# One load of w_down rows split in two, its lower half on eight DMA engines, with the FFN columns permuted to match

## The chip, the cores and the metric

The kernel runs on one core of a Trainium2 chip. The metric is the device time in microseconds (us), measured over whole executions; the profile is of one of these executions. The time before is 188.97 us, the median of 3 runs (188.87 to 189.1).

## The reference

One decode step of a transformer block with adaptive layer norm, for two rows (B = 2, one token each) of width D = 640, in bfloat16. Cut to what matters:

```python
mod = (silu(c) @ w_mod).reshape(2, 6, 1, 640)          # sa, ca, ga, sb, cb, gb
h = layernorm(x) * (1 + ca) + sa
q = (h @ wq) as 32 heads of 192
scores = q @ k_cache[:, :, -1024:].T * 192 ** -0.5
o = softmax(scores) @ v_cache[:, :, -1024:]
x = x + ga * (o @ wo)
h = layernorm(x) * (1 + cb) + sb
x = x + gb * ((gelu(h @ w_gate) * (h @ w_up)) @ w_down) # w_gate, w_up: 640 x 1536; w_down: 1536 x 640
```

The weights and the used part of the caches are 77 MB, each byte of which is used for two rows at most: all of it must come from HBM once.

## The kernel before, in words

The program is written as a list of operations, each for one engine (TensorE "pe", VectorE "dve", ScalarE "act", GpSimd "pool", SyncE "sp"), with the buffers that it reads and writes. A small scheduler works out from these which semaphores each operation waits for, and emits each engine's list in the order in which it was written. It moves nothing: the order of the work is that of the text.

All large loads are issued by SyncE, through one helper (`k_dma`, L266), in this order: w_mod; two pieces of wq; then K and V of 16 groups (four heads of one batch row each) in turn, through a ring of eight slots; three pieces of wo; then w_gate, two pieces of w_up (`WU_SPLIT`), four pieces of w_down (`WD_SPLIT`); and at the very end the store of the result. The FFN weights go to the buffer `r3`, which held w_mod before. Each load covers 128 partitions; each piece has a semaphore of its own, which a DMA raises by 16 in all.

The attention part multiplies K by q on VectorE (L490), sums on TensorE by matmuls with an identity matrix (L502), takes the softmax on VectorE and ScalarE, and multiplies by V on TensorE (L551). wo follows (L622), then the second layer norm (from L392 on).

The FFN is what the change touches. The F = 1536 hidden columns are dealt out as `f = 12 p + r`: partition p of w_down's buffer `wd_v` holds its rows 12 p to 12 p + 11, so that each load takes whole runs of a partition's rows; a piece of `WD_SPLIT` is (first r, count): rows 9 to 11 first, then 0 to 4, 5 to 7, and 8. Gate and up (function `ffn_gu`, matmuls at L655) have to put hidden column `12 p + r` where the transpose will bring it to partition p. They run over five k steps of 128; in each, four matmuls of 384 columns, in four column groups of the array (`tile_position`), make the columns `r = 3 i` to `3 i + 2` of all 128 p for i = 0 to 3: their order within group i is `(m r)`, m being p. ScalarE takes GELU of gate (L661), VectorE multiplies by up (L664), `a_T` (L672) transposes with twelve matmuls, VectorE copies the result to `aT` (L676). Then w_down (L684): for each of its pieces and each row number `fc` in it, four matmuls of 160 columns, which accumulate over all twelve `fc`. VectorE scales (L689) and adds the residual (L691), and SyncE stores.

So the engines' order at the end is, on TensorE: gate; up, first piece (three k steps); up, second piece (two k steps); `a_T`; `down0` to `down3`, each waiting for its own piece. `HP` is 64, `FR` is 3, `FC` is 12, `NR` is 4 and `FT` is 384.

Of the kernel before, what the change touches and what calls it, by code (L numbers as in the profile page):

```python
# [119 lines left out]
def bass_adaLN_cond__sliding_block_cached__geglu_ffn__decode_kernel(  # L120
# [14 lines left out]
    P = 128  # L135
    B, _, D = A_x.shape
# [4 lines left out]
    KT = D // P  # L141
    NQ = H * Dh
    NR = 4
# [8 lines left out]
    FR = 3  # L152
    FC = F // P
# [23 lines left out]
    HP = P // 2  # L177
# [4 lines left out]
    FT = F // NR  # L182
# [4 lines left out]
    with es:  # L187
        S = _Sched(nc, es)
# [40 lines left out]
        h2T = sb("h2T", [P, KT, B], BF16)  # L229
# [11 lines left out]
        aT = sb("aT", [P, FC, RM], BF16)  # L241
        fin = sb("fin", [P, DR], F32)
        finb = sb("finb", [P, DR], BF16)
        ps = es.enter_context(nc.psum_tensor("ps", [P, 8, 512], F32))
# [3 lines left out]
        BK_OT = 6  # L248
# [4 lines left out]
        def bank(k):  # L253
            return ("bank", k)
# [5 lines left out]
        sem_wu = [S.sem("d_wu%d" % i) for i in range(len(WU_SPLIT))]  # L260
        sem_wd = [S.sem("d_wd%d" % i) for i in range(len(WD_SPLIT))]
        sem_ring = [S.sem("d_ring%d" % i) for i in range(NS)]
        sem_out = S.sem("d_out")

        def k_dma(dst, src):
            return lambda e: e.dma_start(dst, src)  # L266
# [11 lines left out]
        for it in items:  # L278
            m = nslots.get(it, 1)
# [27 lines left out]
        def declare_ring(consumed=()):  # L307
            ring_state["done"].update(consumed)
            while ring_state["next"] < len(items):
                it = items[ring_state["next"]]  # L310
                if not all(h in ring_state["done"] for h in before_of[it]):
# [7 lines left out]
                       writes=["wm"], name="ld_wm")  # L319
# [4 lines left out]
        for nm, t in (("scT", scT), ("oT", oT), ("aT", aT)):  # L324
# [6 lines left out]
             reads=["ones_f"], writes=["ident_f"], name="ident_f")  # L331
        S.op("pool", lambda e: e.tensor_copy(out=ident_b[:, :], in_=ident_f[:, :]),
             reads=["ident_f"], writes=["ident_b"], name="ident_b")
# [3 lines left out]
             reads=["ones_b"], writes=["selrow"], name="selrow")  # L337
# [3 lines left out]
             reads=["ones_b"], writes=["selg"], name="selg")  # L341
        for b in range(B):
# [4 lines left out]
                 reads=["ones_b"], writes=[("selq", b)], name="selq%d" % b)  # L347
# [4 lines left out]
             reads=["ones_b"], writes=["ztmp"], name="ztmp")  # L352
# [6 lines left out]
             reads=["ones_f", "bcL"], writes=["bcL"], name="bcLh")  # L359
# [5 lines left out]
             reads=["bcR"], writes=["bcR"] + [("bcR", z) for z in range(2)], name="bcRd")  # L365
# [4 lines left out]
             reads=["ident_f"], writes=["mask_h"], name="mask_h")  # L370
        S.op("dve", lambda e: e.tensor_reduce(out=st32[:, :], in_=ident_f[:, :].rearrange("p (i m) -> p m i", m=32), axis=AX.X, op=ALU.add),
             reads=["ident_f"], writes=["st32"], name="st32")
# [3 lines left out]
             reads=["st32"], writes=["selstat"], name="selstat")  # L376
# [3 lines left out]
        def c_T(e):  # L380
            last = None
            for j in range(KT):
# [4 lines left out]
             reads=[bank(BK_T)], writes=["scT"], name="silu")  # L387
        S.op("dve", lambda e: e.tensor_copy(out=X[:, :], in_=xr[:, :]),
             reads=["xr"], writes=["X"], name="x_f32")
# [20 lines left out]
        def ln_mod(tag, opc_idx, s_idx, dst_bf):  # L410
# [7 lines left out]
            def f(e):  # L418
# [14 lines left out]
             reads=["mask_h"], writes=["maskc"], name="maskc")  # L433
        S.op("dve", lambda e: e.tensor_reduce(out=zsel[:, :, X0:X0 + P].rearrange("p q (h m) -> p q h m", m=32)[:, :, :, 0],
                                              in_=ztmp[:, :, :, :].rearrange("p i q h -> p q h i"), axis=AX.X, op=ALU.max),
             reads=["ztmp", "zsel"], writes=["zsel"], name="zsel")

        mod_pe = []
        for half in range(2):
            def f(e, half=half):  # L440
                last = None
                for k in range(KT):
                    wv = wm_v[:, k, :].rearrange("p (m i n) -> p m i n", i=NR, n=DR)
                    for i in range(NR):
                        last = e.matmul(ps[32 * i:32 * i + RM, half, 0:MH].rearrange("p (m n) -> p m n", n=DR), lhsT=scT[:, k, :],  # L445
                                        rhs=wv[:, 3 * half:3 * half + 3, i, :],
                                        start=(k == 0), stop=(k == KT - 1), tile_position=(0, 32 * i))
                return last
# [3 lines left out]
                 reads=[bank(half)], writes=[("modR", half)], name="mod%d_evac" % half)  # L452
            S.op("dve", lambda e, half=half: e.tensor_scalar(out=opc[:, half, :], in0=modR[:, 3 * half + 1, :], scalar1=1.0, scalar2=None, op0=ALU.add),
                 reads=[("modR", half)], writes=[("opc", half)], name="opc%d" % half)
# [17 lines left out]
        for n in range(NQB):  # L472
            if n % 2 == 0:
                S.op("act", lambda e, n=n: e.activation(out=qrow[:, n * QW:(n + 1) * QW], in_=ps[:, n, :], func=ACTF.Copy),  # L474
                     reads=[bank(n)], writes=[("qrow", n)], name="q1_evac%d" % n)
            else:
                S.op("dve", lambda e, n=n: e.tensor_copy(out=qrow[:, n * QW:(n + 1) * QW], in_=ps[:, n, :]),  # L477
                     reads=[bank(n)], writes=[("qrow", n)], name="q1_evac%d" % n)
        for u, (n, b) in enumerate((n, b) for n in range(NQB) for b in range(B)):
            bk = BK_T + u % 4  # L480
            S.op("pe", lambda e, n=n, b=b, bk=bk: e.matmul(ps[:, bk, :], lhsT=selq[:, b, :], rhs=qrow[:, n * QW:(n + 1) * QW], start=True, stop=True),
                 reads=[("selq", b), ("qrow", n)], writes=[bank(bk)], name="q2_%d_%d" % (n, b))
            S.op("act", lambda e, n=n, b=b, bk=bk: e.activation(out=qbc[:, b, n * QW:(n + 1) * QW], in_=ps[:, bk, :], func=ACTF.Copy),  # L483
                 reads=[bank(bk)], writes=[("qbc", b, n)], name="q2_evac%d_%d" % (n, b))
# [98 lines left out]
        for g in range(NG + 2):  # L583
# [23 lines left out]
            if prev:  # L607
# [5 lines left out]
             reads=[bank(BK_OT)], writes=["oT"], name="oT")  # L613
        for ci, (t0, n) in enumerate(WO_SPLIT):
            def f(e, ci=ci, t0=t0, n=n):
# [13 lines left out]
        r3_dead = [wm_dma] + mod_pe  # L629
        S.dma("sp", k_dma(wg_v.rearrange("p k n -> p (k n)"), B_w_gate.rearrange("(p k) n -> p (k n)", k=KT)), sem_wg,  # L630
              writes=["wg"], deps=r3_dead, name="ld_wg")
        for ci, (k0, nk) in enumerate(WU_SPLIT):
            S.dma("sp", k_dma(wu_v[:, k0:k0 + nk, :].rearrange("p k n -> p (k n)"), B_w_up.rearrange("(p k) n -> p (k n)", k=KT)[:, k0 * F:(k0 + nk) * F]), sem_wu[ci],
                  writes=[("wu", ci)], deps=r3_dead, name="ld_wu%d" % ci)
        wd_src = B_w_down.rearrange("(p r) n -> p (r n)", r=FC)
        for ci, (r0, nr) in enumerate(WD_SPLIT):
            dst, src = wd_v[:, r0:r0 + nr, :].rearrange("p r n -> p (r n)"), wd_src[:, r0 * D:(r0 + nr) * D]
            S.dma("sp", k_dma(dst, src), sem_wd[ci], writes=[("wd", ci)], deps=r3_dead, name="ld_wd%d" % ci)

        S.op("dve", lambda e: e.memset(ps[:, 0:2, :], 0.0), writes=[bank(0), bank(1)], name="init_G")  # L640
        S.op("dve", lambda e: e.tensor_tensor(out=lnt[:, :], in0=ps[:, BK_M, 0:DR], in1=modR[:, 2, :], op=ALU.mult),  # L641
             reads=[bank(BK_M), ("modR", 0)], writes=["lnt"], name="ga_attn")
        S.op("dve", lambda e: e.tensor_tensor(out=X[:, :], in0=lnt[:, :], in1=X[:, :], op=ALU.add),
             reads=["lnt", "X"], writes=["X"], name="x1")
# [3 lines left out]
        def ffn_gu(bk, wv, name, splits):  # L648
            for ci, (k0, nk, key) in enumerate(splits):
                def f(e, k0=k0, nk=nk):  # L650
                    last = None
                    for k in range(k0, k0 + nk):
                        wk = wv[:, k, :].rearrange("p (m i r) -> p i m r", i=NR, r=FR)
                        for i in range(NR):
                            last = e.matmul(ps[32 * i:32 * i + B, bk, 0:FT].rearrange("p (m r) -> p m r", r=FR), lhsT=h2T[:, k, :],  # L655
                                            rhs=wk[:, i, :, :], start=(k == 0), stop=(k == KT - 1), tile_position=(0, 32 * i))
                    return last
                S.op("pe", f, reads=["ln2_out", key], writes=[bank(bk)], name="ffn_%s%d" % (name, ci))

# [2 lines left out]
             reads=[bank(0)], writes=["gl"], name="gelu")  # L662
        ffn_gu(1, wu_v, "up", [(k0, nk, ("wu", ci)) for ci, (k0, nk) in enumerate(WU_SPLIT)])
        S.op("dve", lambda e: e.tensor_tensor(out=aR[:, :], in0=ps[:, 1, 0:FT], in1=gl[:, :], op=ALU.mult),  # L664
             reads=[bank(1), "gl"], writes=["aR"], name="geglu")

        def a_T(e):
            last = None
            for i in range(NR):
# [7 lines left out]
             reads=[bank(2)], writes=["aT"], name="aT")  # L677
        for ci, (r0, nr) in enumerate(WD_SPLIT):
            def f(e, r0=r0, nr=nr):
                last = None  # L680
                for fc in range(r0, r0 + nr):
                    wv = wd_v[:, fc, :].rearrange("p (i n) -> p i n", i=NR)
                    for i in range(NR):
                        last = e.matmul(ps[32 * i:32 * i + RM, BK_OT, CY:CY + DR], lhsT=aT[:, fc, :], rhs=wv[:, i, :],  # L684
                                        start=(fc == WD_SPLIT[0][0]), stop=(fc == WD_SPLIT[-1][0]), tile_position=(0, 32 * i))
                return last
            S.op("pe", f, reads=["aT"] + [("wd", ci)], writes=[bank(BK_OT)], name="down%d" % ci)

        S.op("dve", lambda e: e.tensor_tensor(out=fin[:, :], in0=ps[:, BK_OT, CY:CY + DR], in1=modR[:, 5, :], op=ALU.mult),  # L689
             reads=[bank(BK_OT), ("modR", 1)], writes=["fin"], name="gb_y")  # L690
        S.op("dve", lambda e: e.tensor_tensor(out=finb[:, :], in0=fin[:, :], in1=X[:, :], op=ALU.add),  # L691
             reads=["fin", "X"], writes=["finb"], name="outR")
        S.dma("sp", k_dma(out[:, 0, :].rearrange("b (i n) -> i b n", i=NR), finb[0:P:RB, :]),
              sem_out, reads=["finb"], name="st_out")
# [35 lines left out]
```

## Time and profile before

| | |
|---|---|
| median of 3 runs | 188.97 us (188.87 to 189.1) |
| the profiled execution's own time | 188.87 us |
| its span, first to last instruction | 187.6 us |
| moved by DMA | 77.03 MB, mean 411 GB/s |
| TensorE busy | 107.5 us (57%), 1039 matmuls, mean granted clock 0.901 |
| VectorE busy | 98.2 us (52%) |
| ScalarE busy | 29.9 us (16%) |
| load of w_down rows 9 to 11, 5 to 7: 480 KB each | 30.6 us from issue to landing (median of the two) |
| gate matmuls | 175.51, for 1.89 us |
| last DVE step, then the store's issue | 185.52, then 185.87 |

How to read it: the span is what the profiler saw between the first and the last instruction; the time of an execution is a little longer, since something lies around the span. "Busy" is the time in which an engine had an instruction running; with three engines half busy or more, shares alone do not tell what sets the end. The chain of work that ended last does: it goes back from the last instruction, at each step to what released it. In a line of the timeline the columns are the start and the duration in us, the engine, the line of the kernel, the operation and its operands, the number of instructions merged, and in brackets how long the engine had been idle before and what ended that. A load's time "to landing" runs from its issue to the last of the 16 increments of its semaphore, and includes its time in the queue behind earlier loads.

### The profile page before, as it was taken

The page shows a single profiled execution, that of the slowest core. Times are in us where ns is not written, and L with a number is a line of the kernel's source. Part 1 is how long each engine was busy: PE and PEld are TensorE (multiplying, and loading weights), DVE is VectorE, ACT ScalarE, POOL GpSimd, SP SyncE. Part 2 cuts the span into 40 slices and gives each one's busy share as a digit, 9 for nine tenths or more (in the row PEclk, how much of TensorE's full clock was granted, in tenths as well). Part 3 has the DMA queues.
Part 4 walks back from the last instruction along what each step waited for, and adds up shares of the span by engine and source line. Part 5 has one row for each costly group of instructions (what it writes and reads, how often), then busy time and mean ns, then how long its engine had stood idle before and what let it go on. Part 6 is the DMA issues. An engine that isn't in the chain of part 4 may idle for free.

```text
span 187.6 us, 2409 instructions
## 1 busy us (share of the span) xinstructions
PE 107.5 (57%) x1039; PEld 51.1 (27%) x1039; DVE 98.2 (52%) x147; ACT 29.9 (16%) x72; POOL 5.1 (3%) x23
## 2 busy tenths in 40 slices
PE   0014730742968887676676655675497395364462
PEld 0011200210323443333423323233253152353121
DVE  6131100019588988886595695775865933003211
ACT  3041100082001221112011110210120103103400
POOL 8200000000000000000000000000000000000000
PEclk9999999997587999999879999999969967569696
DMA  7999998999999999999999999999999999999991
GB/s 254 402 451 435 430 459 372 422 435 424 430 422 422 427 425 426 427 424 420 419 432 432 422 423 422 421 438 422 424 423 422 419 488 428 416 384 442 398 396 45
DMA packets 6518, 77.03 MB, mean 411 GB/s; under 512 B 746, under 2 KB 876, under 8 KB 1516
## 3 DMA queue, kind: packets, MB, share of 16 engines
q1 hardware_dynamic: 6492, 76.88, 97.1%
q8 instruction: 8, 0.13, 0.3%
q10 hardware_dynamic: 16, 0.01, 0.0%
q14 instruction: 2, 0.02, 0.0%
HBM read 76.88 MB, written 0.00 MB: 410 GB/s over the span
## 4 chain that ended last, share of the span: by engine, by line
DMA 71%; DVE 15%; PE 7%; ACT 2%; SPq 2%; issue 1%
DMA ring<-in_A_k_cache_dram 37%; DMA ring<-in_A_wq_dram 17%; DMA r<-in_B_w_down_dram 17%; DVE prod L490 9%; PE ps L502 4%; DVE S_sb L509 4%; PE ps L467 2%; SPq L266 2%; ACT qbc L483 2%; DVE ps L485 1%; DVE M L512 1%; ACT qrow L474 1%; PE ps L526 0%; DVE bcR L519 0%; PE ps L684 0%
## 5 line engine op out<-in xcount | busy, mean ns | idle before, releaser
L490 DVE TENSOR_TENSOR prod<-ring,qbc 128x3072 bf16<-128x3072 bf16 x32 | 55.9, 1751 | 14.3 <-DMA ring<-in_A_k_cache_dram 14.3
L502 PE MATMUL ps<-prod,ident_b 128*128 128x512 bf16 x192 | 52.9, 419 | 14.4 <-DVE prod L490 14.4
L502 PEld LDWEIGHTS ps<-prod,ident_b 128*128 128x128 bf16 x192 | 17.5, 104 | 40.2 <-DVE prod L490 17.5
L509 DVE TENSOR_REDUCE S_sb<-ps 128x32 f32<-128x1024 f32 x16 | 19.3, 1206 | 2.1 <-PE ps L502 2.1
L526 PE MATMUL ps<-bcR,bcL 5*128 5x4 f32 x32 | 6.1, 258 | 21.9 <-DVE bcR L519 21.9
L563 ACT ACTIVATE On<-ps,rden 128x384 bf16<-128x384 f32 x16 | 9.3, 580 | 43.5 <-DVE rden L561 21.1
L551 PE MATMUL ps<-ring,E_sb 128*8 128x384 bf16 x256 | 15.5, 369 | 0.0
L534 ACT ACTIVATE E_sb<-Sb_sb 128x128 bf16<-128x128 f32 x16 | 5.0, 310 | 56.4 <-DVE Sb_sb L531 56.4
L467 PE MATMUL ps<-ring,hT 128*2 128x512 bf16 x60 | 6.7, 626 | 9.8 <-DMA ring<-in_A_wq_dram 8.8
L526 PEld LDWEIGHTS ps<-bcR,bcL 5*128 5x128 f32 x32 | 4.7, 183 | 26.1 <-DVE bcR L519 26.1
L477 DVE CAST qrow<-ps 128x512 bf16<-128x512 f32 x1 | 0.7, 692 | 15.7 <-PE ps L467 15.7
L622 PE MATMUL ps<-ring,oT 128*17 128x160 bf16 x192 | 5.5, 294 | 5.6 <-DMA ring<-in_A_wo_dram 5.6
L531 DVE TENSOR_TENSOR Sb_sb<-S_sb,ps 128x128 f32<-128x128 f32 x16 | 4.6, 287 | 7.6 <-PE ps L526 7.6
L540 PEld LDWEIGHTS ps<-denp,maskc 128*128 128x128 f32 x32 | 7.1, 224 | 3.7 <-ACT E_sb L534 0.9
L641 DVE TENSOR_TENSOR lnt<-ps,modR 128x160 f32<-128x160 f32 x1 | 0.3, 325 | 12.6 <-PE ps L622 12.6
L445 PE MATMUL ps<-r,scT 128*17 128x480 bf16 x40 | 4.3, 597 | 3.9 <-DMA r<-in_w_mod_dram 3.9
L622 PEld LDWEIGHTS ps<-ring,oT 128*17 128x17 bf16 x192 | 4.9, 117 | 6.2 <-DMA ring<-in_A_wo_dram 6.2
L551 PEld LDWEIGHTS ps<-ring,E_sb 128*8 128x8 bf16 x256 | 5.1, 90 | 3.7 <-issue 1.2
L396 PE MATMUL ps<-st,selstat 128*128 128x2 f32 x4 | 0.9, 298 | 8.6 <-ACT sqj L392 8.6
L467 PEld LDWEIGHTS ps<-ring,hT 128*2 128x2 bf16 x60 | 1.7, 114 | 14.7 <-DMA ring<-in_A_wq_dram 9.7
L576 PE MATMUL ps<-On,zsel 128*128 128x96 bf16 x64 | 5.2, 241 | 0.7 <-ACT On L563 0.7
L540 PE MATMUL ps<-denp,maskc 128*128 128x1 f32 x32 | 5.1, 230 | 0.8 <-ACT E_sb L534 0.8
(81 smaller groups left out, 71.2 us busy)
## 6 DMA issues: line engine op xcount, KB each, us to landing
ring<-in_A_k_cache_dram SPq DMA_DIRECT2D x16, 1536.0 KB, 24.4
ring<-in_A_v_cache_dram SPq DMA_DIRECT2D x16, 1536.0 KB, 24.2
r<-in_w_mod_dram SPq DMA_DIRECT2D x1, 4800.0 KB, 14.3
ring<-in_A_wq_dram SPq DMA_DIRECT2D x1, 4608.0 KB, 32.3
ring<-in_A_wo_dram SPq DMA_DIRECT2D x1, 4480.0 KB, 23.4
ring<-in_A_wq_dram SPq DMA_DIRECT2D x1, 3072.0 KB, 21.2
ring<-in_A_wo_dram SPq DMA_DIRECT2D x1, 2720.0 KB, 24.1
r<-in_B_w_gate_dram SPq DMA_DIRECT2D x1, 1920.0 KB, 25.0
```

What stands on the lines that cost most here:

```text
L467: last = e.matmul(ps[32 * i:32 * i + B, n, :], lhsT=hT[:, k, :], rhs=wv[:, kk, i, n * QW:(n + 1) * QW], start=(k == 0), stop=(k == KT - 1) ...
L490: S.op("dve", lambda e: e.tensor_tensor(out=prod[:, 2 * (g % 2) + ci, :, :], in0=ring[:, sl, ci * JC * Dh:(ci + 1) * JC * Dh].rearrange("p ...
L502: last = e.matmul(o_ap, lhsT=ident_b[:, :], rhs=prod[:, pz, :, t * GC:(t + 1) * GC], start=(t == 0), stop=(t == NCH - 1))
L509: S.op("dve", lambda e: e.tensor_reduce(out=S_sb[:, z, :], in_=ps[:, 2 * z:2 * z + 2, :].rearrange("p k (j c) -> p (k j) c", c=GC), axis=A ...
L526: S.op("pe", lambda e: e.matmul(ps[:, BK_T, P:P + HQ], lhsT=bcL[:, :], rhs=bcR[:, z, :], start=True, stop=True), reads=[("bcR", z), "bcL"] ...
L531: S.op("dve", lambda e: e.tensor_tensor(out=Sb_sb[:, z, :, :], in0=S_sb[:, z, :].unsqueeze(2).broadcast_to([P, J, HQ]), in1=ps[:, BK_T, P: ...
L534: S.op("act", lambda e: e.activation(out=E_sb[:, z, :, :], in_=Sb_sb[:, z, :, :], func=ACTF.Exp, scale=SCALE, accum_out=denp[:, z:z + 1]), ...
L540: S.op("pe", lambda e: e.matmul(ps[:, BK_T, P + 16:P + 17], lhsT=maskc[:, :], rhs=denp[:, z:z + 1], start=True, stop=True), reads=[("denp" ...
L551: last = e.matmul(ps[32 * i:32 * i + 2 * HQ, BK_O, 0:ON], lhsT=E_sb[:, z, 2 * jp:2 * jp + 2, :].rearrange("p j h -> p (j h)"), rhs=ring[:, ...
L563: S.op("act", lambda e: e.activation(out=On[:, quad % 2, b, :], in_=ps[:, BK_O, 0:ON], func=ACTF.Identity, scale=rden[:, z:z + 1]), reads= ...
L576: last = e.matmul(ps[:, BK_OT, 0:B * NT].rearrange("p (b t) -> p b t", b=B), lhsT=zsel[:, jj, x:x + P], rhs=On[:, quad % 2, :, jj * Dh + d ...
L622: last = e.matmul(ps[32 * i:32 * i + RM, BK_M, 0:DR], lhsT=oT[:, t, :], rhs=wv[:, tl, i, :], start=(t == 0), stop=(t == NT - 1), tile_posi ...
```

## The change

Only the first piece of w_down, rows 9 to 11 (`r0 >= FC - FR`), is loaded in another way, and what depends on where its rows lie. In place of one DMA of 128 partitions there are two. The first fills partitions 0 to 63; its source is written as `(m e) n -> e m n` with e = 8, so its outermost size is 8, and partition `8 e + m` gets the rows of source partition `8 m + e`: the lower 64 partitions are permuted for these three rows. The second fills partitions 64 to 127 in the old order, with a semaphore of its own (`sem_wdh`); `down0` waits for both.

The hidden values have to be permuted in the same way for r = 9 to 11, the fourth column group of gate and up. Its matmul of 384 columns is replaced by two of 192: the first takes the weights of the lower 64 partitions' columns in the order `(a m r)`, the second those of the upper 64 in the old order. That is 50 matmuls in place of 40.

```diff
+        sem_wdh = S.sem("d_wdh")
...
-            S.dma("sp", k_dma(dst, src), sem_wd[ci], writes=[("wd", ci)], deps=r3_dead, name="ld_wd%d" % ci)
+            if r0 >= FC - FR:
+                S.dma("sp", k_dma(dst[0:HP, :], src[0:HP, :].rearrange("(m e) n -> e m n", e=8)), sem_wd[ci],
+                      writes=[("wd", ci)], deps=r3_dead, name="ld_wd%d" % ci)
+                S.dma("sp", k_dma(dst[HP:P, :], src[HP:P, :]), sem_wdh, writes=[("wdh", ci)], deps=r3_dead, name="ld_wdh%d" % ci)
+            else:
+                S.dma("sp", k_dma(dst, src), sem_wd[ci], writes=[("wd", ci)], deps=r3_dead, name="ld_wd%d" % ci)
...
-                        for i in range(NR):
+                        for i in range(NR - 1):
                             last = e.matmul(ps[32 * i:32 * i + B, bk, 0:FT].rearrange("p (m r) -> p m r", r=FR), lhsT=h2T[:, k, :],
                                             rhs=wk[:, i, :, :], start=(k == 0), stop=(k == KT - 1), tile_position=(0, 32 * i))
+                        i = NR - 1
+                        e.matmul(ps[32 * i:32 * i + B, bk, 0:FT // 2].rearrange("p (a m r) -> p a m r", a=8, r=FR), lhsT=h2T[:, k, :],
+                                 rhs=wk[:, i, 0:HP, :].rearrange("p (m a) r -> p a m r", a=8), start=(k == 0), stop=(k == KT - 1),
+                                 skip_group_check=True, tile_position=(0, 32 * i))
+                        last = e.matmul(ps[32 * i:32 * i + B, bk, FT // 2:FT].rearrange("p (m r) -> p m r", r=FR), lhsT=h2T[:, k, :],
+                                        rhs=wk[:, i, HP:P, :], start=False, stop=(k == KT - 1),
+                                        skip_group_check=True, tile_position=(0, 32 * i))
...
-            S.op("pe", f, reads=["aT"] + [("wd", ci)], writes=[bank(BK_OT)], name="down%d" % ci)
+            S.op("pe", f, reads=["aT"] + [("wd", ci)] + ([("wdh", ci)] if r0 >= FC - FR else []), writes=[bank(BK_OT)], name="down%d" % ci)
```

## The prediction

> **What bounds the kernel now.** I read the page first: the share of the DMA queues, then the chain that ended last.
>
> ```profile
> q1 hardware_dynamic: 6492, 76.88, 97.1%
> q8 instruction: 8, 0.13, 0.3%
> ...
> DMA 71%; DVE 15%; PE 7%; ACT 2%; SPq 2%; issue 1%
> ```
>
> The loads keep the 16 DMA engines 97.1% busy, and 71% of the chain is transfer: the bytes set the time. Only eight packets carry instructions, but each holds one engine, and that matters below. Next, the chain in order of time, at its end:
>
> ```profile
> 152.72 31.64 DMA r<-in_B_w_down_dram
> 184.37 0.04 issue
> 184.41 0.72 PE ps L684 x16
> 185.13 0.02 issue
> 185.16 0.34 DVE fin L689
> ```
>
> The reader is to see that the chain goes straight from a w_down load to the last matmuls: since 152.72 nothing else has counted. Last, the timeline of that stretch, which tells how much slack each piece before it has:
>
> ```profile
> 178.19 1.21 PE L655 MATMUL ps<-r,h2T 128*2 128x384 bf16 x12 [0.79 <-DMA r<-in_B_w_up_dram]
> ...
> 180.10 0.86 PE L655 MATMUL ps<-r,h2T 128*2 128x384 bf16 x8 [0.70 <-DMA r<-in_B_w_up_dram]
> ...
> 182.47 0.39 PE L684 MATMUL ps<-r,aT 128*17 128x160 bf16 x12 [0.30 <-DVE aT L676]
> ...
> 183.26 0.53 PE L684 MATMUL ps<-r,aT 128*17 128x160 bf16 x20 [0.41 <-DMA r<-in_B_w_down_dram]
> ...
> 184.41 0.70 PE L684 MATMUL ps<-r,aT 128*17 128x160 bf16 x16 [0.62 <-DMA r<-in_B_w_down_dram]
> ```
>
> Of the four w_down pieces only the first waits for DVE; the others wait for their load. So the end is the landing of the last load plus a fixed tail (185.13 - 184.75 on PE, two DVE steps, the store).
>
> A load lands when the last engine that carries it is done. The trace's semaphore records hold one increment per engine. For the last two loads (rows 5 to 7, and row 8 of w_down) the sixteen come at, in us:
>
> ```
> rows 5-7  182.49 182.50 182.53 182.58 182.60 182.71 183.00 183.27 183.43 | 183.97 184.00 184.07 184.13 184.14 184.19 184.36
> row 8     182.92 182.94 182.97 182.99 183.01 183.10 183.38 183.64 183.84 | 184.37 184.40 184.45 184.54 184.55 184.57 184.75
> ```
>
> Nine engines are early, seven late, and the gap between the groups is 0.53 us. For w_mod, the first load, all sixteen lay within 14.08 to 15.14 and fourteen within 0.44 us. So lateness is collected on the way. I followed it through the packet records: on one engine a packet starts within some ns of the end of the one before. A 16 KB instruction packet (eight, at 26.6, 67.0, 88.9, 111.5, 140.3, 166.4, 173.5 and 182.8) takes some 1.0 to 1.1 us, and the load packet behind it is 0.46 to 0.55 us slow: 1.5 us per packet. The first seven fell on seven different engines, which are the seven late ones; the eighth came when its engine had finished. Two 8 KB ones (72.1, 119.9) cost 0.7 to 1.0 us on two of the early nine.
>
> **The change part by part.**
>
> *The load of rows 9 to 11.* Before, each engine carries 8 rows of 3840 B. These rows follow each other at 146 ns (149 ns in the packet records, less an overlap of 3); from landing to landing it is 179.30 - 178.12 = 1.18 us on the first engine and 181.25 - 180.06 = 1.19 on the last. After, partitions 0 to 63 are one DMA whose source has 8 as its outer size, so 8 engines take 8 rows each, and partitions 64 to 127 a second one, 4 rows on each of 16. The trace shows that the outer size sets the number: the store, outer size 4, has one increment at 186.94 and four at 187.54 to 187.58, where loads of 128 rows have sixteen. So eight engines carry 12 rows and eight carry 4: four rows, 4 x 146 = 0.59 us, move from the one group to the other. [...]
>
> *Are the eight the early ones?* The x load (outer size 4) used four engines, and if a DMA on few engines always starts from the same one, these four are among the eight. For two of them I can follow the chain of packets to the end with little doubt: neither gets a 16 KB packet. For the other two, chains run within 4 ns of each other and may be swapped. That no late engine was hit twice speaks for a fixed round over one set of eight. I take it that the eight that get more rows are among the nine early ones. Then the early end at most at 183.84 + 0.59 = 184.43, the late at 184.75 - 0.59 = 184.16. The last landing moves from 184.75 to 184.43: **-0.32 us**. If the engine of 183.84 is the ninth and not one of the eight, the last is 183.64 + 0.59 = 184.23: -0.52. Rows 5 to 7 would then land at 183.43 + 0.59 = 184.02 at the latest, before 184.36, so their 12 matmuls (0.38 us, 184.41 to 184.79) are over by 184.45 and the last four wait for the last landing, as now.
>
> *One more issue and its wait.* SP's issues of this sort take 0.43 us when not held up; the four w_down issues take 10.69 us from 151.78, since the queue is full. The last is out at 162.47 and its data move from about 182: 20 us cover a 0.43 us step, or even another held-up one (7.7 us). Next on SP is the store, which waits for DVE until 185.87. Cost 0. The first w_down matmul waits for a second semaphore; it starts at 182.47 after aT, and the rows landed at 181.25 (after: 180.30 + 0.59 = 180.9, or 181.25 - 0.59). Behind it on PE are the other three pieces, and DVE's L689 after them; the wait ends 1.2 us before it counts. Cost 0.
>
> *Ten more matmuls.* Each of five k steps, in gate and in up, gets 5 matmuls in place of 4, the last column group in two halves of 192 columns. Gate: 20 in 1.89 us; up: 12 in 1.21 and 8 in 0.86. The halves stream the same columns, so the least is 0; the most is a full record (504 ns) for each, 2.5 us for gate, which no row speaks for, since 20 run in 1.89 us, 95 ns each. I take 95 ns: gate +0.5, up +0.3 and +0.2. Gate ends at 177.40 and the next weights come at 178.15: 0.75 covers it. The first part of up ends at 179.40 and waits until 180.06: covered. The last part delays geglu, aT and the first w_down piece by 0.2: 182.86 + 0.2 = 183.06, still before 183.22, when the next load lands now (about 182.86 after: 182.27 + 0.59). Then even a lost wait leaves 20 matmuls (0.53) done by 183.6, before 184.02. Cost 0; with the cover gone, 0.2. The twenty added PE instructions (with their weight loads) move the eighth instruction packet a little ahead of 182.8, into the time when early engines still work; on one of the eight it would cost 1.5 us. I count that under the second rival.
>
> **The sum.** Profiled execution: span 187.6, time 188.87, so 1.27 lie around the span. 188.87 - 0.32 = 188.55, or - 0.52 = 188.35. That execution is 0.10 below the median of the runs, 188.97; on that footing it is 188.65 and 188.45. I forecast the middle, **188.55**.
>
> **Rivals.**
>
> *The second half's load slows its neighbours (slower).* Before, every load covers all 128 partitions, each engine its own eight. After, 16 engines write the upper 64 partitions at once. No row here shows two engines on one set of partitions. From below it costs nothing; the nearest row of two streams on one path is a k-cache packet beside an instruction packet, 1120 ns at most where 464 is usual, 2.4 times. If two engines halve each other's rate, the four shared rows take 1.17 in place of 0.59, and the late group loses what it was given: the early end at 183.84 + 1.17 = 185.01 at the latest, **+0.26: 189.2**. If the eight rows of the first DMA share too, each engine has 2.34 - 1.17 more: 183.10 + 2.34 = 185.44 for most, +0.69, 189.6. It decides as soon as the twelve rows take over 0.9 us more than eight did before (183.84 + 0.91 = 184.75). Against it: the engines are out of step by up to 1.8 us, so not all meet. I take no cost, by the row that shows each engine at its own even rate (464 ns beside fifteen others), and keep the rest for the range. [...]
>
> *One of the eight is late already.* Then its end is 184.37 to 184.75 + 0.59 = 184.96 to 185.34: +0.21 to +0.59, 189.2 to 189.55. For it: only two of the eight are identified. Against: seven packets on seven engines, none of them these two. Here also belongs the moved eighth packet: 182.94 + 0.59 + 1.5 = 185.03 on an early engine that is still loading.
>
> *Nothing moves:* if the first DMA were spread over 16 engines after all, the sum is as before, 188.97. Against: the store's four increments.
>
> **Chances.** What a measurement here can tell from no change is about 0.2%, 0.38 us: below 188.59 is faster, over 189.35 slower. Forecast 0.46 (0.33 faster, 0.13 within). Shared partitions 0.34 (0.14 within, 0.20 slower). A late engine among the eight 0.14 (0.06 within, 0.08 slower). Nothing moves 0.06 (0.05 within, 0.01 faster). Together 0.34 faster, 0.38 within, 0.28 slower. The range goes from the better forecast with some room, 188.3, to near the dearer end of the first rival, 189.5; left out is that rival's upper tail and a gain over 0.6.
>
> **What would show it.** Right: the sixteen increments of row 8 close up, the late ones near 184.0 to 184.2 and the early ones up to 184.4, and the last group of L684 starts 0.3 us earlier after its wait. Rows of 3840 B at 149 ns in both new DMAs. First rival: 3840 B packets near 300 ns, and the late group still at 184.4 to 184.75. Second: one increment 0.5 us behind the rest. The forecast is wrong altogether if PE no longer waits for a load before its last matmuls.

## The result, and the profile after

The changed kernel takes 191.38 us (median of 4 runs, 191.28 to 191.69), beside 188.92 us (median of 4) for the kernel before: ratio 1.0133, 95% interval 1.0115 to 1.015, **2.46 us slower**. The profiled execution took 191.28 us with a span of 190.0 us. The forecast was 188.55, the range ended at 189.5.

First the page after, the lines of the DMA queue and of the chain that ended last.

```profile
q1 hardware_dynamic: 6500, 76.88, 97.1%
q8 instruction: 8, 0.13, 0.3%
...
DMA 71%; DVE 15%; PE 7%; ACT 2%; SPq 2%; issue 1%
```

The reader is to see that nothing shows here. The queue has eight packets more, the same bytes, and the same 97.1% of a longer span; the table further down shows a share of 1.03 to 1.05 at 241 to 247 GB/s, where it was 0.99 to 1.01 at 403 to 410 before, so time in which a packet is held up counts as busy. The shares of the chain are the same to the per cent. Next, its end, in order of time.

```profile
153.62 33.11 DMA r<-in_B_w_down_dram
186.72 0.04 issue
186.77 0.75 PE ps L697 x14
187.51 0.02 issue
187.54 0.34 DVE fin L702
```

The chain has the same shape, from a w_down load into the last matmuls, but the load lands at 186.72 where it was 184.37. From there on the tail is as long as before (187.51 - 186.77, and DVE). So 2.35 us are in the loads. The timeline of TensorE tells where they begin.

```profile
181.37 0.52 PE L661 MATMUL ps<-r,h2T 128*2 128x384 bf16 x3 [2.10 <-DMA r<-in_B_w_up_dram]
...
183.95 0.58 PE L697 MATMUL ps<-r,aT 128*17 128x160 bf16 x12 [0.50 <-DMA r<-in_B_w_down_dram]
185.60 0.85 PE L697 MATMUL ps<-r,aT 128*17 128x160 bf16 x20 [1.07 <-DMA r<-in_B_w_down_dram]
186.77 0.72 PE L697 MATMUL ps<-r,aT 128*17 128x160 bf16 x16 [0.32 <-DMA r<-in_B_w_down_dram]
```

The second part of up starts at 181.37, not at 180.10: its load, which the change did not touch and which stands in the queue *ahead* of the split one, is 1.27 us late already. The pieces of w_down follow 1.48, 2.34 and 2.36 us later than before. A table by stretches of time shows the rate. Its columns are the stretch, its length, the busy time of PE, weight loads, DVE, ACT and POOL, the granted TensorE clock, the DMA share and the GB/s. First the kernel before, then the changed one.

```profile
176.00:178.00 2.00, 1.41 (x19) 0.35 (x8) 0.00 (x0) 0.49 (x1) 0.00 (x0) 0.53 1.01 420
178.00:180.00 2.00, 1.21 (x12) 0.31 (x12) 0.00 (x0) 0.00 (x0) 0.00 (x0) 1.00 0.99 403
180.00:182.00 2.00, 1.16 (x19) 0.41 (x20) 0.56 (x1) 0.00 (x0) 0.00 (x0) 1.00 1.01 410
```

```profile
176.00:178.00 2.00, 1.91 (x25) 1.10 (x25) 0.00 (x0) 0.03 (x1) 0.00 (x0) 0.50 1.02 416
178.00:180.00 2.00, 1.22 (x15) 0.55 (x15) 0.00 (x0) 0.47 (x1) 0.00 (x0) 0.50 1.05 247
180.00:182.00 2.00, 0.64 (x10) 0.27 (x10) 0.00 (x0) 0.00 (x0) 0.00 (x0) 0.87 1.03 241
182.00:184.00 2.00, 0.75 (x19) 0.47 (x20) 0.76 (x2) 0.00 (x0) 0.00 (x0) 0.99 0.98 294
```

The last two columns are the finding: the DMA engines count as busy all the time, and from 178 to 182 they move 241 to 247 GB/s in place of 403 to 410. In these four microseconds alone (403 - 247) x 2 + (410 - 241) x 2 = 650 KB are left undone, 1.6 us at 410 GB/s. The packet records say who is slow. The first packets of the split load start at 177.57. From 178.0 to 183.0 the trace has 249 packets of the loads, and *all* 249 take over 1.25 times their normal duration ("slow" from here on). With the two ends of the middle four fifths, and the median of before in brackets: rows of 3840 B take 234 to 284 ns (149), of 6144 B, which belong to the load ahead, 391 to 435 (236), of 6400 B, which belong to the one behind, 333 to 445 (248). After 183.5, none does. The sixteen increments for row 8 come at

```
184.51 184.90 185.07 185.61 185.62 185.72 185.87 185.96 186.04 186.22 186.25 186.30 186.35 186.61 187.08 187.13
```

There are no two groups any more, and the last comes 2.38 us after the 184.75 of before.

### The profile page after: what moved, and what is told of

It is laid out like the page before. It is cut to its first block, busy times and chain, and to the rows that moved or that the text cites. A ratio compares the mean times of both kernels' runs of the same rounds, so it can differ in the third digit from the quotient of the medians.

```text
span 190.0 us, 2430 instructions
## 1 busy us (share of the span) xinstructions
PE 108.7 (57%) x1049; PEld 53.2 (28%) x1049; DVE 98.1 (52%) x147; ACT 29.9 (16%) x72; POOL 5.1 (3%) x23
## 3 DMA queue, kind: packets, MB, share of 16 engines
q1 hardware_dynamic: 6500, 76.88, 97.1%
## 4 chain that ended last, share of the span: by engine, by line
DMA 71%; DVE 15%; PE 7%; ACT 2%; SPq 2%; issue 1%
DMA ring<-in_A_k_cache_dram 36%; DMA r<-in_B_w_down_dram 17%; DMA ring<-in_A_wq_dram 17%; DVE prod L491 9%; PE ps L503 4%; DVE S_sb L510 4%; SPq L267 2%; PE ps L468 2%; ACT qbc L484 2%; DVE ps L486 1%; DVE M L513 1%; ACT qrow L475 1%; PE ps L527 0%; DVE bcR L520 0%; PE ps L697 0%
## 5 line engine op out<-in xcount | busy, mean ns | idle before, releaser
L503 PE MATMUL ps<-prod,ident_b 128*128 128x512 bf16 x192 | 54.0, 426 | 13.5 <-DVE prod L491 13.5
L552 PE MATMUL ps<-ring,E_sb 128*8 128x384 bf16 x256 | 14.5, 350 | 0.0
L623 PE MATMUL ps<-ring,oT 128*17 128x160 bf16 x192 | 6.1, 313 | 7.5 <-DMA ring<-in_A_wo_dram 7.5
L623 PEld LDWEIGHTS ps<-ring,oT 128*17 128x17 bf16 x192 | 5.4, 124 | 8.0 <-DMA ring<-in_A_wo_dram 8.0
L661 PE MATMUL ps<-r,h2T 128*2 128x384 bf16 x30 | 4.0, 503 | 2.5 <-DMA r<-in_B_w_up_dram 2.1
```

Of the source, the lines that this page charges most:

```text
L503: last = e.matmul(o_ap, lhsT=ident_b[:, :], rhs=prod[:, pz, :, t * GC:(t + 1) * GC], start=(t == 0), stop=(t == NCH - 1))
L552: last = e.matmul(ps[32 * i:32 * i + 2 * HQ, BK_O, 0:ON], lhsT=E_sb[:, z, 2 * jp:2 * jp + 2, :].rearrange("p j h -> p (j h)"), rhs=ring[:, ...
L623: last = e.matmul(ps[32 * i:32 * i + RM, BK_M, 0:DR], lhsT=oT[:, t, :], rhs=wv[:, tl, i, :], start=(t == 0), stop=(t == NT - 1), tile_posi ...
```

## The experiments

**Theories.** *Shared partitions*: an engine that writes partitions which another engine writes too slows that one, and others with it. *Source order*: reading the lower half in permuted order slows all reads from HBM. *Matmuls*: the ten more matmuls, or the fetch of their instructions. Times are medians; "before" is the kernel before in the same comparison.

| kernel | us | before | ratio, 95% interval |
|---|---|---|---|
| changed kernel | 191.38 | 188.92 | 1.0133 (1.0115 to 1.015) |
| pe_only | 189.02 | 188.90 | 1.0007 (0.9998 to 1.0017) |
| halves_plain | 191.30 | 188.90 | 1.0135 (1.0118 to 1.0152) |
| extra_all | 189.65 | 189.04 | 1.0034 (1.0019 to 1.0049) |
| extra_up16 | 191.36 | 189.04 | 1.0138 (1.0118 to 1.0158) |
| extra_low8 | 192.07 | 188.90 | 1.0166 (1.0151 to 1.0181) |
| extra_own8 | 189.88 | 188.90 | 1.0055 (1.0038 to 1.0071) |
| extra_hi8 | 192.50 | 189.13 | 1.0189 (1.0172 to 1.0206) |
| own_low | 191.15 | 189.13 | 1.0111 (1.0096 to 1.0126) |
| halves_row8 | 189.45 | 189.13 | 1.0019 (1.0009 to 1.0028) |
| front_all | 190.08 | 188.96 | 1.0057 (1.0042 to 1.0072) |
| front_halves | 191.47 | 188.96 | 1.0141 (1.012 to 1.0162) |
| extra_four | 189.22 | 188.92 | 1.0007 (0.9998 to 1.0017) |

### The matmuls alone: pe_only

```diff
-                        for i in range(NR):
+                        for i in range(NR - 1):
...
+                        i = NR - 1
+                        e.matmul(ps[32 * i:32 * i + B, bk, 0:FT // 2].rearrange("p (m r) -> p m r", r=FR), lhsT=h2T[:, k, :],
+                                 rhs=wk[:, i, 0:HP, :], start=(k == 0), stop=(k == KT - 1), ...)
+                        last = e.matmul(ps[32 * i:32 * i + B, bk, FT // 2:FT].rearrange("p (m r) -> p m r", r=FR), lhsT=h2T[:, k, :],
+                                        rhs=wk[:, i, HP:P, :], start=False, stop=(k == KT - 1), ...)
```

> The kernel before with the fourth column group's matmul in two halves of 192 columns, in the old column order, and the old single load. Shared partitions (engines that write partitions another engine also writes slow each other): no change, 188.7 to 189.1. Source order (the permuted read of the lower half slows the reads of all): no change. Matmuls (the ten more matmuls, or the fetch of their instructions, are the loss): near the 191.4 of the changed kernel.

Measured: 189.02, +0.12, not told from no change. The matmul theory falls.

### Two plain halves: halves_plain

```diff
+            if r0 >= FC - FR:
+                S.dma("sp", k_dma(dst[0:HP, :], src[0:HP, :]), sem_wd[ci], writes=[("wd", ci)], ...)
+                S.dma("sp", k_dma(dst[HP:P, :], src[HP:P, :]), sem_wdh, writes=[("wdh", ci)], ...)
...
```

> The kernel before with rows 9 to 11 in two loads of 64 partitions each, both in the old order, so each spread over 16 engines; old matmuls. Every engine has the same bytes as before. Shared partitions: slower by 1.5 to 2.5 us, 190.4 to 191.4, with 3840 B packets at 250 ns or more and neighbours slowed too. Source order: no change, 188.7 to 189.2, packets at 149 ns. Matmuls: no change.

Measured: 191.30, +2.40. From 178.0 to 183.0, 242 of 246 packets are slow. The source order theory falls: here the rows are read in the old order, and the loss is that of the changed kernel. It is also the changed kernel without its point, since here each engine carries eight rows as before (the changed kernel's load of the upper 64 partitions, of the same form, has sixteen increments, 179.12 to 183.82: four rows on each engine, here twice): the shift of four rows bought nothing that can be told (191.38 beside 191.30).

### Which half, and whose partitions: extra_all, extra_up16, extra_low8, extra_own8, extra_hi8

Each is the kernel before with one more load of 240 KB between w_up and w_down, into a buffer of its own that nothing reads, so that only the form of the load differs. `xs` is the source of rows 9 to 11.

```diff
+        # extra_all: 128 partitions, half the width
+        S.dma("sp", k_dma(scr[:, 0:FR * D // 2], xs[:, 0:FR * D // 2]), ...)
+        # extra_up16: upper 64 partitions, as in the change
+        S.dma("sp", k_dma(scr[HP:P, :], xs[HP:P, :]), ...)
+        # extra_low8: lower 64 partitions, as in the change
+        S.dma("sp", k_dma(scr[0:HP, :], xs[0:HP, :].rearrange("(m e) n -> e m n", e=8)), ...)
+        # extra_own8: p0 = 0 and 32; extra_hi8: p0 = 64 and 96
+        S.dma("sp", k_dma(scr[p0:p0 + 32, :], xs[p0:p0 + 32, :].rearrange("(m e) n -> e m n", e=8)), ...)
```

> The control by bytes: the kernel before, which also loads half of the width of rows 9 to 11 (1920 B per row) on all 128 partitions, 8 rows per engine, into a buffer that nothing reads. As many bytes as each of the other extra loads. All theories: +0.6 us, 189.5 to 189.6, packets of 1920 B at about 80 ns.

> The kernel before, which also loads the upper 64 partitions of rows 9 to 11 once more, as the changed kernel does (64 partitions over 16 engines, 4 rows each, old order), into a buffer that nothing reads. If nothing slows down: four rows per engine, +0.59 us, 189.5. Shared partitions: +1.5 us or more, 190.4 and up, with packets of 250 ns or more on all engines. Source order: +0.59, since this read is in order.

> The kernel before, which also loads the lower 64 partitions of rows 9 to 11 once more, in the changed kernel's form (outer size 8, permuted source), into a buffer that nothing reads. Eight engines have 8 rows of 3840 B more, 1.17 us. If nothing slows down: the end is the later of 183.84 + 1.17 and, if one of the eight is a late engine, 184.75 + 1.17, so +0.3 to +1.2 us, 189.2 to 190.1. Shared partitions, if an engine gets 8 neighbouring partitions here and 4 + 4 in a full load: +2 us or more, 191 and up. Source order: +2 us or more as well.

> As extra_low8, but the extra lower half comes as two loads of 32 partitions with outer size 8, permuted source, so that an engine gets 4 partitions of the first 32 and the 4 that lie 32 higher. Same bytes on the same eight engines. Shared partitions: if those are the partitions an engine has in a full load, nothing is shared and only the bytes cost, +0.3 to +1.2 us, 189.2 to 190.1, packets at 149 ns. Source order: as extra_low8, +2 us or more, packets at 250 ns or more.

> As extra_own8, but the two extra loads of 32 partitions go to partitions 64 to 95 and 96 to 127: the same eight engines, the same bytes, each engine alone on its 4 + 4 partitions within the load, but these are partitions that another engine writes in every full load beside it. Shared partitions with whatever load: 191 and up, packets of 250 ns or more. Shared only within one load: as extra_own8, 189.9, packets at 149 ns.

Measured: the bytes alone cost 0.61 (extra_all). The same bytes on the upper half alone cost 2.32, 1.71 more. On the lower half, from the same permuted source, the cost is 3.17 in one load of 64 partitions and 0.98 in two of 32. That these loads go to the same eight engines, an engine taking one index of the outer size, is the author's reading: the increments (eight as data land in the changed kernel, eight for a load of extra_own8) show how many engines, not which. By this reading, besides the number of loads, the only difference is which engine writes which partitions: eight neighbours each in the first, four and the four that lie 32 higher in the second. Engine e even reads the same source rows in both, e, e + 8 and so on to e + 56, so where an engine reads does not make the difference. The same two loads of 32, moved to the upper partitions, cost 3.37, so it is not the number of loads either: there, by the same reading, each engine is alone within the load, but another engine writes these partitions in the loads beside it. The table by stretches for extra_low8, then extra_own8, then extra_hi8:

```profile
178.00:180.00 2.00, 1.55 (x16) 0.24 (x12) 0.00 (x0) 0.49 (x1) 0.00 (x0) 0.50 1.02 218
180.00:182.00 2.00, 0.39 (x8) 0.10 (x8) 0.00 (x0) 0.00 (x0) 0.00 (x0) 0.79 1.03 291
```

```profile
178.00:180.00 2.00, 1.78 (x22) 0.55 (x12) 0.00 (x0) 0.49 (x1) 0.00 (x0) 0.87 1.01 412
180.00:182.00 2.00, 1.19 (x20) 0.44 (x20) 0.56 (x1) 0.00 (x0) 0.00 (x0) 1.00 1.04 423
```

```profile
178.00:180.00 2.00, 1.59 (x20) 0.33 (x12) 0.00 (x0) 0.49 (x1) 0.00 (x0) 0.69 1.03 220
180.00:182.00 2.00, 0.17 (x4) 0.10 (x8) 0.00 (x0) 0.00 (x0) 0.00 (x0) 1.00 1.04 241
```

218 and 291, or 220 and 241 GB/s, against 412 and 423, at nearly the same DMA share. In extra_own8 no row of 3840 B takes over 161 ns. So the runs fit an engine of a full load that owns partitions 4 e to 4 e + 3 and 32 + 4 e to 35 + 4 e (for the eight that this load uses; +0.98 where each writes these alone, +3.17 and +3.37 where it writes others), and a sharing with whoever writes there at the time, in whatever load. That the loss goes with the partitions that an engine writes is shown by these runs; whether what two engines share is the partition itself or something that several partitions have in common is not.

extra_low8 shows one thing more. By this fit the eight engines of its extra load own all of the lower 64 partitions, so the other eight write the upper 64 and share with nobody. Yet all 92 packets that start from 178.0 to 180.0 are slow, on all sixteen engines (the DMA share is 1.02), at 1.32 times their normal duration or more. So engines that by the fit share with nobody, called bystanders below, are slowed too.

extra_own8 answers the other question too. The eight increments of its second part come at 179.15, 179.18, 179.35, 179.38, 179.93, 180.24, 180.78 and 181.07. Less the 1.17 us of eight rows, they started at 177.98 to 179.07 (six) and at 179.61 and 179.90 (two). The load ahead had landed on its nine early engines by 179.08, and on its seven late ones from 179.61 on. So **two of the eight are late engines**, as far as starts worked out in this way can tell. The slowest of all sixteen lands row 8 at 185.76 here, 1.01 after the 184.75 of before, and the time rises by as much.

### The lower half put right, the upper as in the change: own_low

```diff
+                for x0 in range(2):
+                    S.dma("sp", k_dma(dst[32 * x0:32 * x0 + 32, :], src[32 * x0:32 * x0 + 32, :].rearrange("(m e) n -> e m n", e=8)), ...)
+                S.dma("sp", k_dma(dst[HP:P, :], src[HP:P, :]), ...)
```

> The changed loads with the lower half as in extra_own8 (two loads of 32 partitions, each engine on its own partitions) and the upper half as in the change (64 partitions over 16 engines); matmuls as before, so the hidden columns of rows 9 to 11 meet permuted rows on the lower 64 partitions, and the output differs in that. If the lower half's sharing is most of the loss: 189.3 to 189.6, what the four rows more cost the late engines among the eight. If the upper half is enough: 190.5 to 191.4, packets slow from the first upper row to the last.

Measured: 191.15, +2.02. This kernel leaves out the matching order of the hidden columns, so its output is not that of the reference; it is read for its loads alone. The upper half is enough. That is no accident of the form: by the fit above, a row that goes to a partition of a late engine, through another engine, is shared by construction.

### How the loss scales: halves_row8, front_all, front_halves, extra_four

```diff
+            # halves_row8
+            if nr == 1:
+                S.dma("sp", k_dma(dst[0:HP, :], src[0:HP, :]), sem_wd[ci], ...)
+                S.dma("sp", k_dma(dst[HP:P, :], src[HP:P, :]), sem_wdh, ...)
...
+        # front_all, ahead of the load of w_mod
+        S.dma("sp", k_dma(scr[:, :], xs[:, :]), ...)
+        # front_halves, at the same place
+        for x0 in range(2):
+            S.dma("sp", k_dma(scr[HP * x0:HP * x0 + HP, :], xs[HP * x0:HP * x0 + HP, :]), ...)
...
+        # extra_four, two loads, between w_up and w_down
+        S.dma("sp", k_dma(scr[HP:HP + 4, x0 * FR * D:(x0 + 1) * FR * D], xs[HP:HP + 4, :]), ...)
```

> The kernel before with only the last piece, row 8 (160 KB, 1280 B rows), in two plain halves; a third of the bytes of halves_plain. Cost by bytes: a third of halves_plain's +2.4, so +0.8, 189.7. Cost by the window (all engines at about 0.57 of their rate from the first engine that enters the halves to the last that leaves them, which is mostly how far the engines are out of step): the spread of 1.5 to 1.8 us lies after most engines are done, so +0.2 to +0.7, 189.1 to 189.6.

> The control for front_halves: the kernel before, which first of all loads rows 9 to 11 once more, on 128 partitions, into a buffer that nothing reads: 8 rows of 3840 B per engine, 1.17 us. All theories: +1.1 to +1.3 us, 190.0 to 190.2.

> As front_all, but the extra load comes as two plain halves of 64 partitions, while the engines are still in step (the sixteen landings of the first load lie within 0.4 us, but for two). Half rate for the halves' own bytes only: 1.17 us more than front_all, 191.2 to 191.4. Window (all engines slow from the first that enters to the last that leaves): little more than that, since the engines are in step, 191.2 to 191.8. A fixed price for a pair of halves, as at the end: 2.4 us more than front_all, 192.5.

> The kernel before, which also loads partitions 64 to 67 of rows 9 to 11 twice more (two loads of 4 partitions, outer size 4), into a buffer that nothing reads. Four engines have two rows of 3840 B more, 0.29 us, and all of them write four partitions that one other engine also writes; 30 KB in all. Only those who share wait: the four, and that one other engine, have slow packets, about 5 of 16 engines, the others stay at their normal durations; +0.3 to +1.0 us by the slowest of the four. All wait: for a stretch of about 1 us or more every packet of all sixteen engines is slow (over 1.25 times its normal duration), and the loss is about the length of that stretch.

Measured: a third of the bytes, in the last piece, cost 0.32, not 0.8. A likely reason is that the increments of its first half come over a long time, from 182.63 to 185.17, so that most engines are done when the last ones reach it. The same 480 KB in halves cost 2.40 at the end of the queue and 191.47 - 190.08 = 1.39 at its front, where the engines are in step (of the sixteen landings of w_mod before, fourteen lie within 0.44 us). Half the rate for their own bytes would be 1.17, and the four times of front_halves run from 191.22 to 192.03, so the run does not tell that theory from the other. From 3.0 to 4.0 us, 41 of 76 packets are slow, and none of 94 in front_all. Both costs fit a loss that goes with the time in which engines are in and out of a half load, and hence with how far they are out of step. That is not shown: at the front the loads beside the halves are others too, with rows of 38400 B.

extra_four does not decide its question: +0.30 in the medians, with an interval of the ratio that takes in 1. Between 178.0 and 179.5, 15 of 113 packets are slow, one of them 712 ns where 248 is normal. The others are slowed little (half of all by 1.07 times or less, a quarter by 1.2 or more). So with 30 KB on four engines most packets are not slow, where in the changed kernel all are; how much bystanders wait seems to depend on how many share, and how long. Why an engine that shares with nobody is slowed stays open.

## Why the prediction was wrong, point by point

**The bound** was right: the last landing of w_down sets the end, and the tail behind it kept its length.

**What the load does** was right: the first DMA's semaphore, which counts to 16 in all, has one record at 152.75, long before data move, and eight as data land (180.33 to 182.67), so eight engines carry it.

**"I take no cost, by the row that shows each engine at its own even rate"** is the step that failed, and it set the sign. That row (464 ns beside fifteen others) shows sixteen engines that, by the fit to the runs above, never meet: in a load of 128 partitions each writes its own eight. It says nothing about engines that do. The first rival named the mechanism but not its size. It charged doubled rows to those who share, +0.26 to +0.69. Measured are +1.71 for the upper half alone (extra_up16 less extra_all) and +2.19 for the lower (extra_low8 less extra_own8), which do not add up in the change (+2.46). What it missed is that bystanders wait too (extra_low8): in the changed kernel all packets are slow from 178.0 to 183.0, and for the first four of these five us the sixteen engines run at some 0.6 of their rate, although the eight rows of the piece took an engine 1.2 us before. Its dearer price also had a slip: it takes 183.10, where most engines end, while the last landing counts, as its cheaper price has it. From 183.84 the same sum gives 183.84 + 2.34 = 186.18, or +1.43, about 190.3, beyond the range; the last landing measured is 187.13. That "the engines are out of step by up to 1.8 us, so not all meet" was counted as relief; the smaller loss of front_halves, in step, speaks against that, without proving the opposite.

**"I take it that the eight that get more rows are among the nine early ones"** failed too. Two are not (extra_own8, its eight taken to be the change's). Without any sharing, by an estimate from extra_own8, whose eight engines carry eight rows more where the change gives them four, the last landing would have moved by 1.01 - 0.58 = +0.43, to about 189.35: the second rival, whose price (+0.21 to +0.59) holds it. The ground for the assumption was thin: two engines followed out of eight.

**The gap between early and late engines** was there to be used: nine early and seven late again in extra_own8 (179.08, then 179.61). That one instruction packet each made the seven late is the prediction's reading, which no run tests. But what an engine lacks at the end is, by the fit, bytes for its own partitions, and with another engine writing some of those beside it, own_low is 2.02 slower than before.

**One more issue, one more wait, ten more matmuls** at no cost: right. pe_only is within 0.12 us. The first w_down matmuls do wait for their load now (0.50 at 183.95), but three landings follow. The eighth instruction packet comes at 184.34 here, while loads still land, and yet no increment of row 8 lies 1.5 us behind the one before it.

## What to carry to other kernels

Near the DMA bound, first try loads that all cover 128 partitions: here 240 KB more cost 0.61 us in that form, and 2.32 on the upper 64 partitions alone. In these runs a load of part of the partitions that, by the fit, put engines on those of others was not just slow itself, it slowed the loads ahead of and behind it on all engines (249 of 249 packets in the changed kernel); one that kept each engine on its own, extra_own8, cost 0.98 us, less than the 1.17 us of its rows. Before moving bytes from late engines to early ones, find out which engines are late (in extra_own8 the increments of a load with outer size 8 pointed to two) and whether the destination allows another engine at all (own_low: +2.02). And when DMA share stays near 1 while the GB/s fall, as here (1.05 at 247, where it was 0.99 at 403), look at the duration of single packets against the same size elsewhere (here 234 to 284 ns against 149).

## What the runs showed of the hardware that was not expected

- Sharing slows engines that share nothing: in extra_low8, where by the fit above only the lower 64 partitions are shared, 92 of 92 packets in two microseconds, by 1.3 to 3 times. In the changed kernel it is 249 of 249 over five microseconds, most by 1.5 to 1.9 times.
- The order of the price: 240 KB cost 0.61 us on 128 partitions, 2.32 on the upper 64 over 16 engines, and 3.37 on the same partitions over eight engines that by the fit do not own them; and 0.98 on the lower 64 over eight engines that by the fit write only their own.
- The same 480 KB in halves cost 1.39 us at the front of the queue, with the engines in step, and 2.40 at its end, with them some 1.8 us apart.
